# Mixture-of-experts stage: expert pairs share one half/half row block, the last 64 input rows of w1 run as a pair of row tiles, and the first expert's layer 1 goes by 128 rows

## The chip, the cores and the metric

One core of one Trainium2 chip runs the whole program in one launch. TensorE (PE) multiplies, VectorE (DVE), ScalarE (ACT) and GpSimd (POOL) work elementwise, SyncE (SP) and POOL issue DMAs. The metric is the time of one execution on the device in microseconds; lower is better. The kernel before was timed three times: 1001.54, 993.71 and 999.69 us, median 999.69 us.

## What is computed

Two parts follow each other. The first is a recurrent token mixer (RWKV-7) over 4 sequences of 768 tokens with 8 heads of 40; its output is reshaped to 3072 rows of 320. The second is a mixture of 8 experts: each row goes to the one expert with the largest gate value.

```python
x = attn_out.transpose(0, 2, 1, 3).reshape(B * S, H * D)      # 3072 x 320
logits = x @ w_gate                                           # 8 experts
expert_idx = np.argmax(logits, axis=1)
gate_w = probs[np.arange(N), expert_idx]                      # softmax weight of the chosen one
for e in range(E):                                            # rows sorted by expert
    h = np.maximum(x_sorted[lo:hi] @ w1[e], 0.0)              # 320 -> 1024
    y_sorted[lo:hi] = h @ w2[e]                               # 1024 -> 320
out = gate_w[:, None] * y_sorted[inv_perm]
```

All is float32. On the given inputs the argmax of the reference gives the eight experts 421, 323, 414, 388, 357, 423, 371 and 375 rows.

## The kernel before, in words

**The mixer** (lines 294 to 755) cuts the sequences into 24 units of work. Every piece of a unit is a `Step` with an engine, a cost and a rank, and the planner `in_order` writes the steps out in the order in which its costs say that they become ready; each engine's order is thereby fixed. PE's helper `mm` is line 385. The last steps of a unit scale its rows by the gate weight (lines 736 and 738, into `xs`) and store 128 rows of 320 to `x_rows` in DRAM (line 744, SP). POOL multiplies the inputs of a unit (lines 451 and 453).

**The router** (lines 758 to 862) runs when the mixer is done. It counts each row's place within its expert and turns it into a slot: expert e owns NJ = 4 blocks of 128 slots (CAP = 512 rows), rows beyond that go to overflow blocks behind the 32 regular ones. The lists `g_idx` (which row to gather into a slot) and `s_idx` (which output row the slot belongs to) come out of it.

**The experts** (lines 865 to 935) are run one after the other. `gather` fetches 128 rows per block with an indirect DMA on POOL. `turn` transposes a block on PE in three pieces (128, 128 and 64 of the 320 inputs) and DVE copies each piece into `xgT` (lines 882 and 883). `layer1` runs, for each of the 8 blocks of 128 hidden units, three matmuls that accumulate over the inputs, two with 128 rows and one with 64, each 512 columns wide (line 891); DVE and ACT take turns in applying the ReLU (lines 896 and 898). `layer2` gives each block of 128 rows 8 matmuls of 320 columns (line 904), a copy on ACT (line 909) and an indirect store on POOL (line 910). The profile shows two PE instructions per float32 matmul and one per transpose. `fetch` loads an expert's w1 and w2 (2.5 MB) through SP's queue into one of three buffers.

**Order.** Outside the mixer the tile framework's scheduler sets each engine's order from the program's order and its own estimates; semaphores hold what isn't ready. The overflow loop (line 938) runs only if an expert has more rows than CAP.

Of the kernel before, what the change touches and what calls it, by code (L numbers as in the profile page):

```python
# [8 lines left out]
F32 = mybir.dt.float32  # L9
# [5 lines left out]
AF = mybir.ActivationFunctionType  # L15
ALU = mybir.AluOpType
PSUM = bass.MemoryType.PSUM
# [6 lines left out]
def kernel(  # L24
# [21 lines left out]
    nc = tc.nc  # L46
    B, NW, _, D, _, NP, CW = packed.shape
    C = 64
# [20 lines left out]
    NJ = 4  # L69
    CAP = NJ * 128  # L70
    NX = -(-(N - CAP) // 128)
    NC = E * NJ + NX
    assert NC <= 128

# [56 lines left out]
    b1off = counted("b1off", [128, E], [[CAP, E]], -1)  # L131
    b2off = counted("b2off", [128, E], [[-CAP, E]], E * CAP - CAP)
# [25 lines left out]
    x_d = nc.dram_tensor("x_rows", (N, Dm), F32, kind="Internal").ap()  # L158
# [3 lines left out]
    def fetch(pool, w1, w2):  # L162
        t1 = pool.tile([128, DB, F], F32, name="w1")
        t2 = pool.tile([128, FB, Dm], F32, name="w2")
        full = Dm // 128
        nc.sync.dma_start(t1[:, :full, :], w1[: full * 128].rearrange("(a p) f -> p a f", p=128))
        if full < DB:
            nc.sync.dma_start(t1[: Dm - full * 128, full, :], w1[full * 128 :])
        nc.sync.dma_start(t2[:], w2.rearrange("(a p) d -> p a d", p=128))
        return t1, t2  # L170
# [124 lines left out]
    with tc.tile_pool(name="ring", bufs=1) as ring, \  # L295
# [42 lines left out]
        r_xs = Ring("xs", [NP, 2, D], 2, 2)  # L338
# [56 lines left out]
        def unit(u):  # L395
# [320 lines left out]
            def two():  # L716
                return psum[:, psx.at : psx.at + 2, : 2 * WX].rearrange("x b (i n) -> x b i n", i=2)
# [14 lines left out]
            for b in range(2):  # L732
                def scaled(e, b=b):
                    dst_, src_ = xs[:, 2 * b : 2 * b + 2], two()[:, b, :, :128].rearrange("x i (a d) -> x i a d", a=2)[:, :, :, :D]
                    if e == ACT:
                        nc.scalar.activation(dst_, src_, AF.Copy, scale=g[:, E:])
                    else:
                        nc.vector.tensor_scalar_mul(dst_, src_, g[:, E:])
                Step(late, ANY, 0.3, scaled, reads=[psx] + hg, writes=hxs[b : b + 1])

            def store(e):
                for q in range(2):
                    r0 = (2 * bh + q) * S + c * C
                    nc.sync.dma_start(x_d[r0 : r0 + C, :], xs[halves[q]].rearrange("x p a d -> x (p a d)"))
# [16 lines left out]
    with tc.tile_pool(name="rps", bufs=1, space=PSUM) as rps_pool:  # L761
# [103 lines left out]
    xg_pool = ctx.enter_context(tc.tile_pool(name="moe_x", bufs=3))  # L865
    wk_pool = ctx.enter_context(tc.tile_pool(name="moe_wk", bufs=2))
    mps_pool = ctx.enter_context(tc.tile_pool(name="moe_ps", bufs=3, space=PSUM))

    def gather(g):
        g["xg"] = xg_pool.tile([128, NJ, Dm], F32, name="xg")  # L870
        for j in range(g["n"]):
            nc.gpsimd.indirect_dma_start(  # L872
                out=g["xg"][:, j, :], out_offset=None,
                in_=x_d[:, :], in_offset=bass.IndirectOffsetOnAxis(ap=g["gi"](j), axis=0),
            )

    def turn(g):
        g["xT"] = wk_pool.tile([128, DB, CAP], F32, name="xgT")
        for j in range(g["n"]):
            tp = mps_pool.tile([128, DB, 128], F32, name="tp", bufs=2)  # L880
            for db, (d0, dsz) in enumerate(dch):
                nc.tensor.transpose(tp[:dsz, db, :], g["xg"][:, j, d0 : d0 + dsz], ident[:])  # L882
                nc.vector.tensor_copy(g["xT"][:dsz, db, j * 128 : (j + 1) * 128], tp[:dsz, db, :])  # L883

    def layer1(g):
        cols = g["n"] * 128
        g["h"] = wk_pool.tile([128, FB, CAP], F32, name="h_sb")
        for fb in range(FB):
            hp = mps_pool.tile([128, CAP], F32, name="hp")
            for db, (d0, dsz) in enumerate(dch):  # L890
                nc.tensor.matmul(  # L891
                    hp[:, :cols], lhsT=g["w"][0][:dsz, db, fb * 128 : (fb + 1) * 128],
                    rhs=g["xT"][:dsz, db, :cols], start=(db == 0), stop=(db == DB - 1),
                )
            if fb % 2 == 0:
                nc.vector.tensor_relu(g["h"][:, fb, :cols], hp[:, :cols])  # L896
            else:
                nc.scalar.activation(g["h"][:, fb, :cols], hp[:, :cols], AF.Relu)  # L898

    def layer2(g):  # L900
        for j in range(g["n"]):
            zp = mps_pool.tile([128, Dm], F32, name="zp", bufs=2)
            for fb in range(FB):
                nc.tensor.matmul(  # L904
                    zp[:], lhsT=g["h"][:, fb, j * 128 : (j + 1) * 128], rhs=g["w"][1][:, fb, :],
                    start=(fb == 0), stop=(fb == FB - 1),
                )
            zo = wk_pool.tile([128, Dm], F32, name="zo", bufs=3)
            nc.scalar.copy(zo[:], zp[:])  # L909
            ins_ = nc.gpsimd.indirect_dma_start(  # L910
                out=out[:, :], out_offset=bass.IndirectOffsetOnAxis(ap=g["si"](j), axis=0),
                in_=zo[:], in_offset=None, bounds_check=N - 1, oob_is_err=False,
            )
            ins_ = getattr(ins_, "ins", ins_)
            if g["apart"]:
                tc.declare_no_dep(ins_, group="rows_out", reason="disjoint rows")
                tc.add_to_no_dep_group("rows_out", ins_)

    def cols_of(t, c0):
        return lambda j: t[:, c0 + j : c0 + j + 1]  # L920

    groups = [dict(n=NJ, gi=cols_of(g_idx, e * NJ), si=cols_of(s_idx, e * NJ), apart=True) for e in range(E)]
    gather(groups[0])
    gather(groups[1])
    turn(groups[0])
    for e, g in enumerate(groups):
        if e + 2 < E:
            gather(groups[e + 2])
        g["w"] = weights.pop(e)
        layer1(g)  # L930
        if e + 1 < E:
            turn(groups[e + 1])
        layer2(g)
        if e + 2 < E:
            weights[e + 2] = fetch(w_pool, moe_w1[e + 2], moe_w2[e + 2])
# [3 lines left out]
    with tc.If(nx > 0):  # L939
        with tc.For_i(0, nx, 1) as i:  # L940
            ex = nc.sync.value_load(xe[0:1, bass.ds(i, 1)], min_val=0, max_val=E - 1)
            gi = wk_pool.tile([128, 2], I32, name="gi")
            nc.vector.tensor_copy(gi[:, 0:1], g_idx[:, bass.ds(i + E * NJ, 1)])
            nc.vector.tensor_copy(gi[:, 1:2], s_idx[:, bass.ds(i + E * NJ, 1)])
# [3 lines left out]
            g = dict(n=1, w=w, gi=lambda j: gi[:, 0:1], si=lambda j: gi[:, 1:2], apart=False)  # L948
            gather(g)
            turn(g)  # L950
            layer1(g)
            layer2(g)
# [34 lines left out]
```

## Time and profile before

| | |
|---|---|
| median of the runs | 999.69 us (993.71 to 1001.54) |
| the profiled execution | 996.33 us |
| its span, first to last instruction | 994.6 us |
| PE busy | 895.2 us (90%), 17804 matmul instructions |
| DVE, ACT, POOL busy | 393.3, 250.3, 172.9 us |
| mean granted TensorE clock | 0.966 |

The span begins with the first instruction and ends with the last one; 1.73 us of the profiled execution lie outside it. Busy shares are means over three stages (mixer to about 616 us, router to about 640 us, experts to the end), so they say little about one stage. In the tables "x" is a number of instructions, a value in square brackets is the idle time before an instruction and what ended it, and "issue" is waiting for nothing that the profile shows.

### The profile page before, as it was taken

To read this page: it belongs to the slowest core of one execution; us is meant where nothing else is said; L and a number is where in the kernel's file an instruction comes from. 1 tells how busy PE (TensorE), PEld (TensorE's weight loads), DVE (VectorE), ACT (ScalarE), POOL (GpSimd) and SP (SyncE) were. 2 spreads that over 40 slices of the span, in tenths; PEclk is the share of its full clock that TensorE was granted. 3 is DMA by queue.
4 is the path that set the end of the run, shared out by engine and by line. 5 is a ranking of instruction groups with operands and counts; after the bars stand their busy time and mean duration, and the time that the engine had idled before them with its cause. 6 is when DMAs were issued, how large, how long until landed. Compare 5 with 4: busy or idle time off the path is not lost. (4 is left out here: it accounts for less than half of the span.)

```text
span 994.6 us, 39246 instructions
## 1 busy us (share of the span) xinstructions
PE 895.2 (90%) x17804; PEld 651.6 (66%) x17804; DVE 393.3 (40%) x801; ACT 250.3 (25%) x508; POOL 172.9 (17%) x206
## 2 busy tenths in 40 slices
PE   0979999999999999989999995299999999999996
PEld 0877788888888888878888884136445363544534
DVE  6436566566555555555545542611201012010110
ACT  0334334333423333333423441001100000011000
POOL 8321202111201111111101000533022030100101
PEclk9999999999989999999989996599999999999998
DMA  5333313222212222222222001721122142212000
GB/s 157 81 78 69 75 43 74 57 57 67 63 37 55 61 57 56 60 54 61 59 48 53 14 11 33 237 62 49 60 89 93 61 123 79 76 60 68 20 0 21
DMA packets 132796, 64.18 MB, mean 65 GB/s; under 512 B 117009, under 2 KB 128275, under 8 KB 132628
## 3 DMA queue, kind: packets, MB, share of 16 engines
q1 hardware_dynamic: 127176, 51.97, 20.5%
q0 software_dynamic: 3072, 9.18, 3.1%
q8 instruction: 140, 2.29, 1.0%
q10 hardware_dynamic: 2380, 0.50, 0.2%
q14 instruction: 28, 0.23, 0.1%
HBM read 53.75 MB, written 9.18 MB: 63 GB/s over the span
## 5 line engine op out<-in xcount | busy, mean ns | idle before, releaser
L891 PE MATMUL hp<-xgT,w 128*128 128x512 f32 (+1 forms) x384 | 191.8, 629 | 0.0
L385 PE MATMUL ps<-X 64*64 64x64 f32 (+1 forms) x6144 | 151.4, 243 | 6.9 <-issue 3.5
L904 PE MATMUL zp<-w,h_sb 128*128 128x320 f32 x512 | 145.0, 433 | 0.0
L891 PEld LDWEIGHTS hp<-xgT,w 128*128 128x128 f32 (+1 forms) x384 | 63.4, 190 | 123.1 <-issue 122.0
L385 PEld LDWEIGHTS ps<-X 64*64 64x64 f32 x6144 | 128.0, 135 | 21.5 <-issue 13.4
L380 ACT COPY X<-ps 128x512 f32<-128x512 f32 x175 | 99.9, 586 | 122.8 <-PE ps L385 116.6
L896 DVE TENSOR_SCALAR h_sb<-hp 128x512 f32<-128x512 f32 x32 | 22.1, 692 | 247.2 <-PE hp L891 247.2
L904 PEld LDWEIGHTS zp<-w,h_sb 128*128 128x128 f32 x512 | 94.6, 191 | 34.5 <-issue 0.8
L451 POOL TENSOR_TENSOR KB<-KB,rv 128x512 f32<-128x512 f32 x48 | 56.6, 1200 | 209.4 <-DMA KB<-in_packed_dram 85.2
L382 DVE COPY X<-ps 128x512 f32<-128x512 f32 x89 | 61.5, 691 | 62.5 <-PE ps L385 62.4
L898 ACT ACTIVATE h_sb<-hp 128x512 f32<-128x512 f32 x32 | 19.1, 597 | 202.8 <-PE hp L891 202.8
L453 POOL TENSOR_TENSOR A<-A,q 128x512 f32<-128x512 f32 x24 | 28.4, 1183 | 231.6 <-PE ps L385 121.7
L910 POOL DMA_INDIRECT out_dram<-zo,s_idx x32 | 31.6, 989 | 181.4 <-ACT zo L909 180.2
L385 PE MATMUL ps<-X,ihalf 64*64 64x256 f32 x768 | 60.6, 377 | 1.1 <-issue 1.1
L436 DVE TENSOR_TENSOR_SCAN rv<-dec,ones 128x521 f32<-128x521 f32 x24 | 29.8, 1244 | 59.2 <-DMA dec<-in_packed_dram 57.7
L385 PE MATMUL ps<-R,Vu 64*128 64x64 f32 x768 | 50.9, 284 | 1.7 <-ACT Vu L644 1.6
L385 PE MATMUL ps<-A,KB 64*128 64x64 f32 x768 | 51.1, 286 | 0.0
L385 PEld LDWEIGHTS ps<-R,Vu 64*128 64x128 f32 x768 | 47.4, 196 | 5.0 <-ACT Vu L644 2.1
L872 POOL DMA_INDIRECT xg<-x_rows,g_idx x32 | 30.7, 959 | 108.6 <-PE tp L882 78.9
L385 PEld LDWEIGHTS ps<-A,KB 64*128 64x128 f32 x768 | 47.7, 198 | 2.3 <-POOL A L453 0.4
L909 ACT COPY zo<-zp 128x320 f32<-128x320 f32 x32 | 13.6, 425 | 134.4 <-PE zp L904 134.4
L467 DVE TENSOR_TENSOR GA<-ps,m_up 128x512 f32<-128x512 f32 x48 | 31.2, 685 | 39.2 <-PE ps L385 39.1
(174 smaller groups left out, 1127.5 us busy)
## 6 DMA issues: line engine op xcount, KB each, us to landing
w<-in_moe_w_dram SPq DMA_DIRECT2D x8, 1280.0 KB
w<-in_moe_w_dram SPq DMA_DIRECT2D x8, 1024.0 KB
KB<-in_packed_dram SPq DMA_DIRECT2D x188, 40.0 KB
dec<-in_packed_dram SPq DMA_DIRECT2D x96, 40.0 KB
V<-in_packed_dram SPq DMA_DIRECT2D x96, 40.0 KB
Vu<-in_packed_dram SPq DMA_DIRECT2D x96, 40.0 KB
x_rows<-xs SPq DMA_DIRECT2D x48, 80.0 KB
A<-in_packed_dram SPq DMA_DIRECT2D x92, 40.0 KB
```

The costliest lines, as they stand in the source:

```text
L380: nc.scalar.copy(dst, src)
L382: nc.vector.tensor_copy(dst, src)
L385: nc.tensor.matmul(out_, lhsT=lhsT, rhs=rhs, start=start, stop=stop, skip_group_check=True)
L436: Step(pre, DVE, 1.4, lambda e: nc.vector.tensor_tensor_scan(rv[:, : SEG * C1 + 1][:, ::-1], dec[:, ::-1], ones65[:, ::-1], 0.0, op0=ALU.m ...
L451: Step(pre, POOL, 1.25, lambda e, kb=kb, by=by: nc.gpsimd.tensor_tensor(kb, kb, by, op=ALU.mult), reads=hrv, writes=hKB[i : i + 1])
L453: Step(pre, POOL, 1.22, lambda e: nc.gpsimd.tensor_tensor(Aq[:], Aq[:], q3[:, :, :C], op=ALU.mult), reads=hq, writes=hA)
L467: Step(u, DVE, 0.69, lambda e, s=s, ps=ps: nc.vector.tensor_tensor(GA[:, s], psum[:, ps.at + s, :].rearrange("x (p q j) -> x p q j", p=NP, ...
L872: nc.gpsimd.indirect_dma_start(out=g["xg"][:, j, :], out_offset=None, in_=x_d[:, :], in_offset=bass.IndirectOffsetOnAxis(ap=g["gi"](j), ax ...
L891: nc.tensor.matmul(hp[:, :cols], lhsT=g["w"][0][:dsz, db, fb * 128 : (fb + 1) * 128], rhs=g["xT"][:dsz, db, :cols], start=(db == 0), stop= ...
L896: nc.vector.tensor_relu(g["h"][:, fb, :cols], hp[:, :cols])
L904: nc.tensor.matmul(zp[:], lhsT=g["h"][:, fb, j * 128 : (j + 1) * 128], rhs=g["w"][1][:, fb, :], start=(fb == 0), stop=(fb == FB - 1),)
L910: ins_ = nc.gpsimd.indirect_dma_start(out=out[:, :], out_offset=bass.IndirectOffsetOnAxis(ap=g["si"](j), axis=0), in_=zo[:], in_offset=Non ...
```

## The change

**Blocks.** NJ becomes 3 and CAP 448: an expert owns three blocks of its own and half of a fourth, which it shares with its partner (experts 0 and 1, 2 and 3, ...). A pair has PB = 7 blocks instead of 8, all four pairs 28 instead of 32. The router's slot arithmetic gets a second threshold.

**Rows of 384.** `x_rows` is 384 wide: POOL copies the last 64 inputs of each row behind them, so that a transposed block holds these 64 twice, in partitions 0 to 63 and 64 to 127. The last 64 rows of w1 are loaded into a tile of their own, `w1c`, even hidden blocks in the lower partitions and odd ones in the upper.

**Layer 1** takes two hidden blocks at a time: four matmuls with 128 rows, then two with 64 rows, one in each half of the array's rows. It is 448 columns wide; expert 0's is cut into four passes of 128, 128, 128 and 64 columns.

**Layer 2** of the shared block lets the first expert's 64 rows fill output partitions 0 to 63 and the second's 64 to 127, by turns. `turn` copies a whole block with one DVE instruction (two for the shared block). Work buffers are three deep instead of two, `hp` has four PSUM buffers instead of three, `xg` holds a pair's seven blocks, two deep.

```diff
-    NJ = 4
-    CAP = NJ * 128
+    NJ = 3
+    PB = 2 * NJ + 1
+    CAP = NJ * 128 + 64
...
-        t1 = pool.tile([128, DB, F], F32, name="w1")
+        t1 = pool.tile([128, DB - 1, F], F32, name="w1")
+        t3 = pool.tile([128, FB // 2, 128], F32, name="w1c")
...
+        for i in range(2):
+            nc.sync.dma_start(
+                t3[i * 64 : (i + 1) * 64], w1[Dm - 64 :].rearrange("p (k i f) -> i p k f", i=2, f=128)[i],
+            )
...
+            Step(late, POOL, 0.2, lambda e: nc.gpsimd.tensor_copy(xs[:, Dm:], xs[:, Dm - 64 : Dm]), reads=hxs[1:2], writes=hxs[2:3])
...
-        gx = sm_pool.tile([128, E, NT], F32)
-        nc.vector.tensor_scalar(gx[:], slot[:], scalar1=CAP + 0.5, scalar2=None, op0=ALU.is_ge)
-        nc.vector.tensor_tensor(gx[:], gx[:], b2[:].unsqueeze(2).to_broadcast([128, E, NT]), op=ALU.mult)
-        nc.vector.tensor_add(slot[:], slot[:], gx[:])
+        nc.vector.tensor_sub(b2[:], b2[:], b3off[:])
+        gx = sm_pool.tile([128, 2, E, NT], F32)
+        for i, (above, by) in enumerate(((NJ * 128, b3off), (CAP, b2))):
+            nc.vector.scalar_tensor_tensor(
+                gx[:, i], in0=slot[:], scalar=above + 0.5, in1=by[:].unsqueeze(2).to_broadcast([128, E, NT]),
+                op0=ALU.is_ge, op1=ALU.mult,
+            )
+        for i in range(2):
+            nc.vector.tensor_add(slot[:], slot[:], gx[:, i])
...
+    def turn(xg, j, *to):
+
+        tp = mps_pool.tile([128, DB, 128], F32, name="tp", bufs=2)
+        for db in range(DB):
+            nc.tensor.transpose(tp[:, db, :], xg[:, j, db * 128 : (db + 1) * 128], ident[:])
+        for xT, r0, n, c0 in to:
+            nc.vector.tensor_copy(xT[:, :, c0 : c0 + n], tp[:, :, r0 : r0 + n])
+
+    def layer1(w, xT, h, c0, c1):
+        for fb in range(0, FB, 2):
+            hps = []
+            for i in range(2):
+                hp = mps_pool.tile([128, CAP], F32, name="hp")
+                hps.append(hp)
+                for db in range(DB - 1):
+                    nc.tensor.matmul(
+                        hp[:, : c1 - c0], lhsT=w[0][:, db, (fb + i) * 128 : (fb + i + 1) * 128], rhs=xT[:, db, c0:c1],
+                        start=(db == 0), stop=False,
+                    )
+            for i in range(2):
+                hf = slice(i * 64, (i + 1) * 64)
+                nc.tensor.matmul(hps[i][:, : c1 - c0], lhsT=w[1][hf, fb // 2, :], rhs=xT[hf, DB - 1, c0:c1], start=False, stop=True)
+            nc.vector.tensor_relu(h[:, fb, c0:c1], hps[0][:, : c1 - c0])
+            nc.scalar.activation(h[:, fb + 1, c0:c1], hps[1][:, : c1 - c0], AF.Relu)
+
+    def layer2(si, *parts, apart=True):
+
+        zp = mps_pool.tile([128, Dm], F32, name="zp", bufs=2)
         for fb in range(FB):
+            r0 = 0
+            for w, h, c0, n in parts:
                 nc.tensor.matmul(
+                    zp[r0 : r0 + n], lhsT=h[:, fb, c0 : c0 + n], rhs=w[2][:, fb, :], start=(fb == 0), stop=(fb == FB - 1),
...
+    turns(0)
+    xgs[1] = gathers(1)
+    for e in range(E):
+        k, i = divmod(e, 2)
+        w = weights[e]
+        h = hs[e] = wk_pool.tile([128, FB, CAP], F32, name="h_sb")
+
+        for c0 in (range(0, CAP, 128) if e == 0 else (0,)):
+            layer1(w, xTs[e], h, c0, min(c0 + 128, CAP) if e == 0 else CAP)
+        if e + 1 < E:
+            turns(e + 1)
+        if i == 1 and k + 2 < E // 2:
+            xgs[k + 2] = gathers(k + 2)
+        for j in range(NJ):
+            layer2(col(k * PB + i * NJ + j), (w, h, j * 128, 128))
+        if i == 1:
+            layer2(col(k * PB + 2 * NJ), *((weights[x], hs[x], NJ * 128, 64) for x in (e - 1, e)))
```

How the instructions stand, at three places. First PE where the experts begin: `tp` is a transposed block, `hp` a layer-1 result, `w_223` (before) and `w_227` (now) the first 256 rows of w1 of expert 0. Before:

```order
L882 MATMUL tp<-ident,xg 128x128 x4
L882 MATMUL tp<-ident,xg 64x128 x2
L882 MATMUL tp<-ident,xg 128x128 x4
L891 MATMUL hp<-xgT,w_223 128x512
L882 MATMUL tp<-ident,xg 64x128 x2
L891 MATMUL hp<-xgT,w_223 128x512 x23
```

Now:

```order
L895 MATMUL tp<-ident,xg 128x128 x9
L906 MATMUL hp<-xgT,w_227 128x128
L895 MATMUL tp<-ident,xg 128x128 x3
L906 MATMUL hp<-xgT,w_227 128x128 x3
L912 MATMUL hp<-xgT,w1c 128x128 x2
```

All four blocks (12 transposes) still stand ahead of layer 1, but for one matmul; layer 1 itself is cut into 128-column pieces.

Second PE at an odd expert (expert 1): its last hidden blocks, the next expert's transposes and layer 2, where `zp` is a layer-2 result and `w_229` and `w_10741` are w2 of experts 0 and 1. Before:

```order
L891 MATMUL hp<-xgT,w_10709 128x512 x24
L882 MATMUL tp<-ident,xg 128x128 x2
L904 MATMUL zp<-w_10710,h_sb 128x320
L882 MATMUL tp<-ident,xg 128x128 x2
L904 MATMUL zp<-w_10710,h_sb 128x320
L882 MATMUL tp<-ident,xg 64x128 x2
```

Now:

```order
L906 MATMUL hp<-xgT,w_10739 128x448 x4
L912 MATMUL hp<-xgT,w1c 128x448 x2
L895 MATMUL tp<-ident,xg 128x128 x6
L922 MATMUL zp<-w_10741,h_sb 128x320
L895 MATMUL tp<-ident,xg 128x128 x6
L922 MATMUL zp<-w_10741,h_sb 128x320 x23
L922 MATMUL zp<-w_229,h_sb 64x320
L922 MATMUL zp<-w_10741,h_sb 64x320
```

The 64-row matmuls stand two by two, transposes go in sixes with one layer-2 matmul between, and the shared block alternates the two experts.

Third POOL in the mixer, two units of work, where `KB` and `A` are scaled inputs of a unit. Before:

```order
L451 TENSOR_TENSOR KB_160<-KB_160,rv_169 128x512 x2
L453 TENSOR_TENSOR A_152<-A_152,q_172 128x512
L451 TENSOR_TENSOR KB_158<-KB_158,rv_168 128x512 x2
L453 TENSOR_TENSOR A_150<-A_150,q_170 128x512
L451 TENSOR_TENSOR KB_159<-KB_159,rv_169 128x512 x2
```

Now:

```order
L459 TENSOR_TENSOR KB_164<-KB_164,rv_173 128x512 x2
L461 TENSOR_TENSOR A_156<-A_156,q_176 128x512
L459 TENSOR_TENSOR KB_162<-KB_162,rv_172 128x512 x2
L751 COPY xs_216<-xs_216 128x64
L461 TENSOR_TENSOR A_154<-A_154,q_174 128x512
L751 COPY xs_217<-xs_217 128x64
```

The copy of the 64 inputs stands among the unit's multiplications, and the store of `x_rows` waits for it. PE's order in the mixer is as it was.

## Rows read from the trace of the kernel before

**Rows 1.** Windows: us, then busy us of each engine, granted clock, DMA share, GB/s.

```profile
647.00:650.00 3.00, 3.00 (x6) 1.15 (x5) 0.49 (x2) 0.00 (x0) 2.39 (x3) 0.53 0.50 130
650.00:671.30 21.30, 21.30 (x44) 6.80 (x42) 2.77 (x4) 1.79 (x3) 5.10 (x6) 1.00 0.19 52
713.63:985.10 271.47, 271.47 (x809) 135.84 (x808) 34.08 (x96) 26.40 (x52) 38.23 (x39) 1.00 0.22 69
985.10:994.60 9.50, 0.00 (x1) 0.00 (x0) 0.00 (x0) 0.42 (x1) 0.98 (x1) 0.64 0.01 1
```

**Rows 2.** Timeline of PE, two experts: start, duration in us, engine, line, instruction.

```profile
690.00 23.70 PE L891 MATMUL hp<-xgT,w 128*128 128x512 f32 x48
...
732.32 23.70 PE L891 MATMUL hp<-xgT,w 128*128 128x512 f32 x48
```

**Rows 3.** Timeline of ACT, two blocks of the last expert's layer 2.

```profile
976.57 0.42 ACT L909 COPY zo<-zp 128x320 f32<-128x320 f32 x1 [3.93 <-PE zp L904]
980.88 0.42 ACT L909 COPY zo<-zp 128x320 f32<-128x320 f32 x1 [3.88 <-PE zp L904]
```

**Rows 4.** Timeline of PE's weight loads in layer 1; two instructions a matmul.

```profile
690.86 0.19 PEld L891 LDWEIGHTS hp<-xgT,w 128*128 128x128 f32 x1 [0.24 <-issue]
691.81 0.29 PEld L891 LDWEIGHTS hp<-xgT,w 64*128 64x128 f32 x2 [0.76 <-issue]
...
693.83 0.19 PEld L891 LDWEIGHTS hp<-xgT,w 128*128 128x128 f32 x1 [0.24 <-issue]
```

**Rows 5.** Timeline of PE in the mixer; rows*columns of the tile, moving shape.

```profile
316.47 0.61 PE L385 MATMUL ps<-GA,ihalf 64*64 64x256 f32 x8
316.90 0.29 PE L385 MATMUL ps<-N,GA 64*64 64x64 f32 x8
...
317.96 2.00 PE L385 MATMUL ps<-R,Vu 64*128 64x64 f32 x32
319.89 1.09 PE L580 MATMUL ps<-ident,Vu 128*128 128x128 f32 x8
...
322.85 1.65 PE L385 MATMUL ps<-ZU,nKB 128*64 128x104 f32 x32
324.42 0.66 PE L571 MATMUL ps<-ident,V 128*128 128x128 f32 x4
```

**Rows 6.** Timeline of PE, two narrow windows: the last two, and the last one, of those 32.

```profile
319.67 0.29 PE L385 MATMUL ps<-R,Vu 64*128 64x64 f32 x2
...
319.69 0.27 PE L385 MATMUL ps<-R,Vu 64*128 64x64 f32 x1
```

**Rows 7.** Chain of work: start, us, what; last gather of expert 0.

```profile
640.68 3.31 DMA xg<-x_rows,g_idx
```

**Rows 8.** Timeline of PE: that block's transposes, and the end of layer 1.

```profile
644.12 0.66 PE L882 MATMUL tp<-ident,xg 128*128 128x128 f32 x2 [0.63 <-DMA xg<-x_rows,g_idx]
...
671.30 0.44 PE L882 MATMUL tp<-ident,xg 128*128 128x128 f32 x2
```

**Rows 9.** Timeline of DVE in the router.

```profile
618.68 0.36 DVE L764 TENSOR_TENSOR sc<-lgn,lmin 128x192 f32<-128x192 f32 x1 [3.02 <-DMA x_rows<-xs]
...
623.26 0.25 DVE L813 TENSOR_SCALAR gx<-slot 128x192 f32<-128x192 f32 x1
...
624.69 0.36 DVE L815 TENSOR_TENSOR slot<-slot,gx 128x192 f32<-128x192 f32 x1
```

**Rows 10.** Timeline of POOL and ACT: a small POOL copy; a unit's scaling and POOL's next work.

```profile
1.69 0.23 POOL L99 COPY ihalf<-ident 64x64 f32<-64x64 f32 x1
...
306.67 0.40 ACT L736 ACTIVATE xs<-ps,g 128x160 f32<-128x160 f32 x1
...
316.13 2.34 POOL L451 TENSOR_TENSOR KB<-KB,rv 128x512 f32<-128x512 f32 x2 [11.12 <-DMA KB<-in_packed_dram]
```

**Rows 11.** Groups of DVE from 600 us on: xcount, busy us, mean ns, idle before.

```profile
L896 DVE TENSOR_SCALAR h_sb<-hp 128x512 f32<-128x512 f32 x32 | 22.1, 692 | 247.2 <-PE hp L891 247.2
```

**Rows 12.** Timeline of SP's queue: a later expert's w2.

```profile
732.52 0.37 SPq L169 DMA_DIRECT2D w<-in_moe_w_dram  x1
```

More of the change, by code (lines that the diff above doesn't have):

```diff
@@ L862 @@
         nc.vector.tensor_copy(s_idx[:], tb[:])
[L865 to L887, printed above, removed]
+    xg_pool = ctx.enter_context(tc.tile_pool(name="moe_x", bufs=2))
@@ new lines, with gather @@
+    wk_pool = ctx.enter_context(tc.tile_pool(name="moe_wk", bufs=3))
+    mps_pool = ctx.enter_context(tc.tile_pool(name="moe_ps", bufs=4, space=PSUM))
+    def gather(xg, j, gi):
+        nc.gpsimd.indirect_dma_start(
+            out=xg[:, j, :], out_offset=None, in_=x_d[:, :], in_offset=bass.IndirectOffsetOnAxis(ap=gi, axis=0),
+        )
[5 more added lines that the diff above has]
+            nc.vector.tensor_copy(xT[:, :, c0 : c0 + n], tp[:, :, r0 : r0 + n])
@@ L895, in layer1 @@
[L895 to L913, printed above, removed]
-            ins_ = getattr(ins_, "ins", ins_)
-            if g["apart"]:
-                tc.declare_no_dep(ins_, group="rows_out", reason="disjoint rows")
-                tc.add_to_no_dep_group("rows_out", ins_)
@@ new lines, in layer2 @@
+                    skip_group_check=True,
+                )
+                r0 += n
+        zo = wk_pool.tile([128, Dm], F32, name="zo")
+        nc.scalar.copy(zo[:], zp[:])
+        ins_ = nc.gpsimd.indirect_dma_start(
+            out=out[:, :], out_offset=bass.IndirectOffsetOnAxis(ap=si, axis=0),
+            in_=zo[:], in_offset=None, bounds_check=N - 1, oob_is_err=False,
+        )
+        if apart:
+            ins_ = getattr(ins_, "ins", ins_)
+            tc.declare_no_dep(ins_, group="rows_out", reason="disjoint rows")
+            tc.add_to_no_dep_group("rows_out", ins_)
@@ new lines, in gathers, with col, turns @@
+    def gathers(k):
+        xg = xg_pool.tile([128, PB, DX], F32, name="xg")
+        for j in (*range(NJ), 2 * NJ, *range(NJ, 2 * NJ)):
+            gather(xg, j, g_idx[:, k * PB + j : k * PB + j + 1])
+        return xg
+    def col(b):
+        return s_idx[:, b : b + 1]
+    xgs = {0: gathers(0)}
+    xTs, hs = {}, {}
+    def turns(e):
+        k, i = divmod(e, 2)
+        if i == 0:
+            for x in (e, e + 1):
+                xTs[x] = wk_pool.tile([128, DB, CAP], F32, name="xgT")
+        for j in range(NJ):
+            turn(xgs[k], i * NJ + j, (xTs[e], 0, 128, j * 128))
+        if i == 0:
+            turn(xgs[k], 2 * NJ, *((xTs[e + a], 64 * a, 64, NJ * 128) for a in range(2)))
@@ L947 @@
             )
[L948 to L952, printed above, removed]
+            xg = xg_pool.tile([128, PB, DX], F32, name="xg")
+            xT = wk_pool.tile([128, DB, CAP], F32, name="xgT")
+            h = wk_pool.tile([128, FB, CAP], F32, name="h_sb")
+            gather(xg, 0, gi[:, 0:1])
+            turn(xg, 0, (xT, 0, 128, 0))
+            layer1(w, xT, h, 0, 128)
+            layer2(gi[:, 1:2], (w, h, 0, 128), apart=False)
 _OUTS = [((3072, 320), 'float32')]
```

56 lines of the change are left out of this document (22 added, 34 removed).

## The prediction

> **What bounds the kernel now.** I read the windows first, because the busy shares are means over three stages. From about 650 us to 985 us PE has no idle time and runs at the full granted clock (1.00, the 2.4 GHz level), while DVE, ACT, POOL and the DMAs are far from full [rows 1]. So in the expert stage the end is set by PE's own stream: whatever is taken out of it is gained one for one, as long as the others keep up. The timeline of PE shows the period of one expert: 732.32 - 690.00 = 42.32 us, of which layer 1 is 23.7 us [rows 2] and the rest, 18.6 us, is layer 2 with the next expert's transposes. Behind the last matmul lie 9.5 us of copy, store and ending [rows 1], which nothing here touches.
>
> **Unit prices.** Two copies of finished layer-2 blocks stand 4.31 us apart [rows 3]. A block is 8 matmuls of 2 instructions and 320 columns: 0.269 us each, 0.84 ns per column and instruction. A 512-column instruction is then 0.430 us. In layer 1 the same weight load comes back after 693.83 - 690.86 = 2.97 us [rows 4], which is one hidden block with 6 instructions, 2.58 us of streaming. The remaining 0.39 us are its two changes of shape (128 rows to 64 and back): before the 64-row load the load queue sits idle for 0.76 us, so weights aren't loaded ahead across a change. One change costs 0.2 us. The 18.6 us less 4 x 4.31 leave 1.4 us for 12 transposes, 0.12 us each.
>
> **Layer 1 of experts 1 to 7.** Two hidden blocks take 8 instructions of 448 columns (0.376 us each, 3.01 us), one pair of 64-row matmuls and two changes (0.4 us). The price of the pair is the open one. One after the other it would be 4 x 0.376 = 1.50 us; with both row tiles at work together it is 0.75 us. Nothing in the trace runs such a pair at this width. The nearest rows are the mixer's. Tiles of 64x64 with 256 columns: 8 instructions from 316.47 to 316.90 [rows 5], 0.43 us, which is exactly two streams of 256 columns, so four tiles, two of them above each other, worked at once. Tiles of 64x128 with 64 columns: 32 instructions in 319.89 - 317.96 = 1.93 us [rows 5], no better than one after the other (32 x 0.054 = 1.72 and a change). That speaks against overlap at first sight, but every such instruction also loads 128 columns of weights, and full-width transposes with 128 columns, right behind, need about as long per load. The last two of them decide for me: one starts at 319.67 and the other at 319.69 [rows 6], 0.02 us apart, which two streams of 0.054 us in one queue could not. I take 0.75 us and keep 1.50 for the range. Then two hidden blocks are 4.16 us and an expert 16.6 us instead of 23.7: 7 x 7.1 = **49.7 us less**.
>
> The Trainium skill, "TensorE: Matmul & The Clock Gate", section "Measured speedup vs the span model", gives only 3.07 times for four row tiles, 77% of full overlap. By that a pair would be about 0.98 us, an estimate, and the sum 938. The trace's 0.43 us for four tiles is full overlap [rows 5], so I stay with it and keep partial overlap as a rival.
>
> **Layer 2.** A pair of experts had 8 blocks and has 7. The shared one runs two 64-column tiles by turns. In the mixer 32 instructions of that kind with 104 columns took 324.42 - 322.85 = 1.57 us [rows 5], 1.37 without the change of shape, where one after the other they would take 2.80. So they overlap fully, and the shared block costs a block's 4.31 us and two changes, 4.7. Saved: 2 x 4.31 - 4.7 = 3.9 us a pair, **15.7 us in all**.
>
> **Transposes.** There are 84 instead of 96, 1.4 us less. But six now come in a row with two buffers, and DVE, still at the ReLU of the last pair (0.69 us for 512 columns [rows 11]), has to copy 384 columns (about 0.54 us by the same rate) before the third block can be turned. One layer-2 matmul of 0.54 us stands between. I put 0.2 us of waiting on each of 7 experts, 1.4 us: **together nothing**.
>
> **Expert 0.** The change's words suggest that it starts with the rows that have arrived. By the order on PE it can't: the transposes of the fourth block stand ahead of all but one of its matmuls, and that block's gather lands last, at 640.68 + 3.31 = 643.99 [rows 7]. Before, layer 1 ended at 671.30 [rows 8], 27.3 us after that. Now: three transposes, 0.8 us (two took 0.66 us at that clock [rows 8]); then four passes. In a pass of 128 columns an instruction is 0.107 us, so two hidden blocks are 10 x 0.107 and two changes, 1.47 us, and a pass 5.9 us. For the pass of 64 columns streaming alone would give 3.7 us; I take 5.9, since the 64-column tiles above went at the pace of their loads. Four passes: 23.5 us, where one pass of 448 would be 16.6. The granted clock is 0.53 between 647 and 650 us and 1.00 after [rows 1], so the first 5 us run at the 1.2 GHz level and lose 2.5 us. In all 26.8 us against 27.3: **0.5 us less**. The cut costs about what the narrower layer 1 would have brought here.
>
> **Ahead of the experts.** The router's first instruction waits for the last store of x_rows [rows 9], and that store now waits for a POOL copy: 0.3 us (a 64x64 copy takes 0.23 [rows 10]). Two router instructions of 0.25 and about 0.36 us become two of about 0.36, plus an addition of 0.36 [rows 9] and a subtraction on 8 columns: 0.6 us. Longer rows in the gather: 0.1 us. **1.0 us more.** Inside the mixer the copy is hidden: ACT's scaling ends at 307.07 and POOL's next multiplication starts at 316.13, held by its own DMA [rows 10]. Without that 9 us of cover each of 24 copies would cost 0.3 us, 7 us in all.
>
> **What must not become late.** The weights: an odd expert's w2 now waits until the shared block of the pair before is done, but is needed only a whole even expert and one layer 1 later, 47 us; before, an expert's w2 was asked for at 732.52 [rows 12] and the DMAs stood at 22% [rows 1]. The third pair's gathers now wait on POOL for expert 1's transposes, with expert 0's stores queued behind them for some 9 us; three output buffers cover that until expert 1's layer 2. Both ReLUs of a pair come at once, each under 0.7 us, and four buffers leave 4 us.
>
> **Sum.** -49.7 - 15.7 + 0 - 0.5 + 1.0 = -64.9 us. The profiled execution took 996.33 us, 0.3% under the median of the runs (999.69): 996.33 - 64.9 = **931 us**. With the change priced at both ends (the 64-column pass at 3.7 us, no transpose wait, no POOL wait), the forecast's own range is 923 to 937.
>
> **Rivals.**
> Row tiles in part or not at all together. For it: the 1.93 us. Against: four tiles at once, and the two starts. Not at all: 28 pairs x 0.75 and 16 narrow ones x 0.21, 24.5 us, 956 us; in between, about 943. Chance 0.12, half of it at each. The skill's 77% is of this kind.
> The cut expert 0 never gets the full clock. Before, the clock rose under dense 512-column streams; now short streams and a change every 0.5 us or so stand there. Against: the mixer's tiles run at the full rate with shorter streams [rows 5]. The other 21 us would take twice as long: 952 us. Chance 0.08.
> Column tiles one after the other: 4 x 4.3 us, 949 us. The 1.57 us speak against it. Chance 0.03.
> Slower than before: the pairs and shape changes keep TensorE at 1.2 GHz through layer 1 of experts 1 to 7. Its 116 us would double, to about 1047 us; it decides from some 65 us of doubled work on, over half of layer 1. For it: the clock did stay low for as long as PE had gaps [rows 1]. Against: layer 1 already changes shape twice every 2.97 us [rows 4] and holds 1.00. Chance 0.02.
> That rows overflow into the loop I leave out: the fullest expert has 423 rows, under 448.
>
> **Chances.** The forecast has 0.72, the rivals 0.25, and 0.03 are for something cheaper still. Faster by over 1% (10 us, about what a measurement of this kernel tells from none): all but the last rival and an unnamed stall, 0.97; within 1%: 0.01; slower: 0.02. The range of 921 to 954 leaves out rows one after the other and the slow case, and reaches down to an expert 0 without its clock loss and its waits.
>
> **What would show it.** Layer 1 of an expert takes 16.6 us in PE's timeline, two 64-row matmuls of a pair start within 0.05 us, finished blocks stay 4.3 us apart with the shared one at 4.7, a pair of experts has a period near 67 us, expert 0's layer 1 ends 26.8 us after its last gather. Layer 1 at 19.6 us would mean row tiles one after the other; idle time of PE behind a DMA or a semaphore in the expert stage would mean that one of the covers failed.

## The result and the profile after

The changed kernel's median is 934.12 us (928.01 to 944.22), beside 1000.62 us for the kernel before: ratio 0.933, 95% interval 0.926 to 0.940. (Ratios and their intervals leave out executions more than 1.5% behind the fastest of their kernel; medians don't.) The forecast was 931 us, its range 921 to 954. The profiled execution took 928.01 us, its span is 926.3 us, 68.3 us less than before; the forecast said 64.9 us less.

Windows of the changed kernel: the beginning of expert 0, the rest of its layer 1, the other experts' matmuls, the end (us, busy us of each engine, granted clock, DMA share, GB/s).

```profile
640.50:649.30 8.80, 7.67 (x32) 6.18 (x32) 2.59 (x6) 0.28 (x1) 6.67 (x8) 0.50 0.56 156
649.40:670.60 21.20, 21.20 (x174) 18.07 (x173) 3.88 (x14) 3.72 (x14) 3.95 (x5) 1.00 0.19 53
684.60:917.30 232.70, 232.70 (x864) 126.69 (x862) 27.98 (x52) 25.84 (x53) 31.32 (x32) 1.00 0.22 73
917.30:926.30 9.00, 0.01 (x2) 0.00 (x0) 0.00 (x0) 0.42 (x1) 0.98 (x1) 0.78 0.01 2
```

As in [rows 1], PE is busy without a gap from expert 1 on, at a granted clock of 1.00. The timeline of PE shows where layer 1 of experts 1 and 2 begins and what follows it:

```profile
684.57 3.17 PE L906 MATMUL hp<-xgT,w 128*128 128x448 f32 x8
687.67 1.02 PE L912 MATMUL hp<-xgT,w1c 64*128 64x448 f32 x4
688.62 3.27 PE L906 MATMUL hp<-xgT,w 128*128 128x448 f32 x8
...
701.09 0.87 PE L895 MATMUL tp<-ident,xg 128*128 128x128 f32 x6
...
720.12 3.27 PE L906 MATMUL hp<-xgT,w 128*128 128x448 f32 x8
...
736.75 0.88 PE L895 MATMUL tp<-ident,xg 128*128 128x128 f32 x6
...
750.76 1.67 PE L906 MATMUL hp<-xgT,w 128*128 128x448 f32 x4
...
767.28 0.88 PE L895 MATMUL tp<-ident,xg 128*128 128x128 f32 x6
```

Layer 1 takes 701.09 - 684.57 = 16.52 us (16.63 behind an odd expert: 736.75 - 720.12), where [rows 2] showed 23.7 (23.63 to the next transpose at 713.63, [rows 1]). A pair of 64-row matmuls takes 688.62 - 687.67 = 0.95 us to the next start. The rest of a period is 19.03 us behind an odd expert (720.12 - 701.09) and 14.01 us behind an even one. Two experts take 767.28 - 701.09 = 66.19 us.

A narrow window of PE's timeline answers to [rows 6]: two instructions, each up to 0.64 us long, lie within 0.65 us, so they started together.

```profile
687.67 0.65 PE L912 MATMUL hp<-xgT,w1c 64*128 64x448 f32 x2
```

ACT's copies of finished blocks answer to [rows 3]; the last of these blocks is the shared one:

```profile
711.51 0.42 ACT L928 COPY zo<-zp 128x320 f32<-128x320 f32 x1 [3.92 <-PE zp L922]
715.81 0.42 ACT L928 COPY zo<-zp 128x320 f32<-128x320 f32 x1 [3.88 <-PE zp L922]
720.31 0.42 ACT L928 COPY zo<-zp 128x320 f32<-128x320 f32 x1 [4.07 <-PE zp L922]
```

Ordinary blocks stay 4.30 us apart, the shared one takes 4.50 us.

Expert 0 and the router: PE's first transposes and the end of expert 0's layer 1, POOL's new copy, and the router's first instruction on DVE (for [rows 8 to 10]). In a pass of 128 columns two hidden blocks take 651.39 - 649.88 = 1.51 us.

```profile
640.51 0.87 PE L895 MATMUL tp<-ident,xg 128*128 128x128 f32 x3 [5.11 <-DMA xg<-x_rows,g_idx]
...
649.88 1.16 PE L906 MATMUL hp<-xgT,w 128*128 128x128 f32 x8
...
651.39 1.16 PE L906 MATMUL hp<-xgT,w 128*128 128x128 f32 x8
...
670.60 0.88 PE L895 MATMUL tp<-ident,xg 128*128 128x128 f32 x6
```

```profile
615.25 0.24 POOL L751 COPY xs<-xs 128x64 f32<-128x64 f32 x1 [21.59 <-DVE xs L747]
```

```profile
618.51 0.36 DVE L776 TENSOR_TENSOR sc<-lgn,lmin 128x192 f32<-128x192 f32 x1 [3.33 <-DMA x_rows<-xs]
```

### The profile page after: what moved, and what is told of

Read it like the earlier page. It is cut to its first block, busy times and chain, and to the rows that moved or that the text cites. A ratio compares the mean times of both kernels' runs of the same rounds, so it can differ in the third digit from the quotient of the medians.

```text
span 926.3 us, 39472 instructions
## 1 busy us (share of the span) xinstructions
PE 829.6 (90%) x17936; PEld 648.6 (70%) x17936; DVE 383.9 (41%) x751; ACT 249.0 (27%) x516; POOL 170.4 (18%) x224
## 4 chain that ended last, share of the span: by engine, by line
PE 40%; issue 34%; DMA 9%; POOL 6%; DVE 5%; SPq 3%; ACT 1%; POOLq 0%; DVEq 0%; ACTq 0%
PE ps L393 36%; DMA dec<-in_packed_dram 8%; PE ps L588 3%; POOL out_dram L929 3%; SPq L428 3%; POOL xg L887 3%; DVE q L452 1%; PE ps L579 1%; ACT TF L388 1%; DVE rv L444 1%; DVE xT L707 0%; DVE ZU L674 0%; DVE oh_c L852 0%; DVE ST L606 0%; DVE oh_r L859 0%
## 5 line engine op out<-in xcount | busy, mean ns | idle before, releaser
L922 PE MATMUL zp<-w,h_sb 128*128 128x320 f32 (+1 forms) x512 | 123.8, 433 | 0.0
L913 DVE TENSOR_SCALAR h_sb<-hp 128x448 f32<-128x448 f32 (+2 forms) x44 | 21.9, 497 | 218.7 <-PE hp L912 218.7
L906 PE MATMUL hp<-xgT,w 128*128 128x448 f32 (+2 forms) x352 | 111.4, 460 | 0.0
L922 PEld LDWEIGHTS zp<-w,h_sb 128*128 128x128 f32 (+1 forms) x512 | 80.6, 177 | 37.5 <-issue 2.4
L906 PEld LDWEIGHTS hp<-xgT,w 128*128 128x128 f32 x352 | 57.9, 196 | 48.8 <-issue 46.6
L929 POOL DMA_INDIRECT out_dram<-zo,s_idx x28 | 27.6, 987 | 185.0 <-ACT zo L928 183.8
L914 ACT ACTIVATE h_sb<-hp 128x448 f32<-128x448 f32 (+2 forms) x44 | 19.4, 442 | 152.7 <-PE hp L912 152.7
L393 PE MATMUL ps<-ZU,nKB 128*64 128x104 f32 (+1 forms) x768 | 41.3, 260 | 6.0 <-DVE ZU L674 5.7
L393 PEld LDWEIGHTS ps<-ZU,nKB 128*64 128x64 f32 x768 | 35.9, 142 | 15.2 <-issue 11.6
```

Of the source, the lines that this page charges most:

```text
L393: nc.tensor.matmul(out_, lhsT=lhsT, rhs=rhs, start=start, stop=stop, skip_group_check=True)
L906: nc.tensor.matmul(hp[:, : c1 - c0], lhsT=w[0][:, db, (fb + i) * 128 : (fb + i + 1) * 128], rhs=xT[:, db, c0:c1], start=(db == 0), stop=False,
L922: nc.tensor.matmul(zp[r0 : r0 + n], lhsT=h[:, fb, c0 : c0 + n], rhs=w[2][:, fb, :], start=(fb == 0), stop=(fb == FB - 1), skip_group_check ...
L929: ins_ = nc.gpsimd.indirect_dma_start(out=out[:, :], out_offset=bass.IndirectOffsetOnAxis(ap=si, axis=0), in_=zo[:], in_offset=None, bound ...
```

## The experiments

The length of the mixer differs by some 10 us from one execution to the next. Its clock falls to 0.50 several times for 3 to 10 us, at other places each time; how much of the difference that makes wasn't worked out. So each single execution is judged from the first transpose of expert 0 to the end of the span, which I call the **stage**: 354.6 us before (639.99 to 994.6), 285.8 us in the changed kernel. The first transpose before:

```profile
639.99 0.45 PE L882 MATMUL tp<-ident,xg 128*128 128x128 f32 x1 [5.02 <-DMA xg<-x_rows,g_idx]
```

**One row tile after the other.** All 64-row tiles in partitions 0 to 63; the load of `w1c` changes to match (not shown here), nothing else:

```diff
-nc.tensor.matmul(hps[i][...], lhsT=w[1][hf, fb // 2, :], rhs=xT[hf, DB - 1, c0:c1], ...)
+nc.tensor.matmul(hps[i][...], lhsT=w[1][:64, fb + i, :], rhs=xT[:64, DB - 1, c0:c1], ...)
```

> The changed kernel, but the last 64 rows of w1 of both hidden blocks lie in partitions 0 to 63, so the two 64-row matmuls of a pair use the same half of the array. Number of instructions, columns and shape changes stay. Theory (in the changed kernel the two row tiles work at the same time): two hidden blocks take 4.9 us instead of 4.16 us at 448 columns, layer 1 of an expert 19.5 us instead of 16.5, and the span grows by 28 x 0.75 + 3.4 for expert 0, from 926.3 to about 951 us. Rival (the pair never overlapped, the gain came from fewer columns and fewer shape changes): 4.16 us and 926 us as before.

983.03 us, a stage of 333.2 us. Its PE timeline in expert 1:

```profile
722.07 1.77 PE L908 MATMUL hp<-xgT,w1c 64*128 64x448 f32 x4
723.77 3.27 PE L903 MATMUL hp<-xgT,w 128*128 128x448 f32 x8
```

A pair costs 1.70 us instead of 0.95: 0.75 us more, exactly two streams of 448 columns. So in the changed kernel the row tiles overlap fully. Two experts take 810.53 - 738.48 = 72.05 us instead of 66.19, so 2.93 us more each. But that explains 8 x 2.93 = 23 us of the 47 by which the stage grew. The rest is in expert 0, where the clock rose only at 707.93:

```profile
651.20:702.20 51.00, 50.35 (x197) 43.76 (x195) 5.58 (x19) 3.99 (x15) 8.51 (x9) 0.50 0.15 40
719.00:733.00 14.00, 14.00 (x36) 6.18 (x35) 1.32 (x3) 1.51 (x3) 0.98 (x1) 1.00 0.03 12
```

PE was busy in 50.35 of 51 us and yet ran at 0.50. This is my second rival, in a kernel that differs from the changed one only in the partitions of those tiles and in their load.

**The old order with 448 columns.** Each hidden block takes its two 128-row matmuls and then its own 64-row one.

```diff
-for fb in range(0, FB, 2): ...  # four matmuls, then the pair
+for fb in range(FB): ...        # two matmuls, then one with 64 rows
```

> Layer 1 in the order of the kernel before at the new width: per hidden block two matmuls with 128 rows and then one with 64 rows, always in partitions 0 to 63; blocks, layer 2 and all else as changed. Theory (overlap of row tiles 0.75 us and two spared shape changes of 0.2 us per two hidden blocks): two hidden blocks 12 x 0.376 + 4 x 0.2 = 5.3 us, layer 1 21.2 us, span about 926.3 + 32 + 10 for expert 0 = 968 us. Rival (the narrower 448 columns are the main gain of layer 1): layer 1 close to 16.5 us and a span within 10 us of 926.

1003.16 us, no faster than before: two experts take 75.20 us, 4.5 us more an expert than in the changed kernel, and expert 0's layer 1 stays at the low clock, 59 us long (653.26 to 712.59):

```profile
653.20:712.60 59.40, 59.03 (x198) 46.11 (x196) 5.58 (x19) 3.99 (x15) 8.51 (x9) 0.50 0.12 34
```

Layer 1 of expert 1 takes 749.23 - 728.16 = 21.07 us here. So of the 7.1 us that the change takes out of an expert's layer 1, the 448 columns bring 23.63 - 21.07 = 2.56 us and the pairs the other 4.5: 2.9 by overlap (the run above) and the rest by fewer changes of shape. What the later experts gained was eaten by expert 0, whose way from the first transpose to the end of layer 1 took 62.4 us instead of 31.3.

**Column tiles apart.** In the shared block the first expert's 8 matmuls, then the second's:

```diff
-for fb in range(FB):
-    for w, h, c0, n in parts:
+for w, h, c0, n in parts:
+    for fb in range(FB):
```

> The shared block's 8 matmuls of the first expert come first and then the 8 of the second, instead of by turns; everything else as changed. Theory (column tiles overlap because neighbours in the queue use different halves of the columns): the shared block takes 8.8 us instead of 4.5, span 926.3 + 4 x 4.3 = 943 us. Rival (a 64-column tile is cheaper by itself, whatever stands next to it): 4.5 us and 926 us.

ACT's copies around the shared block, and PE at its middle:

```profile
733.66 0.43 ACT L928 COPY zo<-zp 128x320 f32<-128x320 f32 x1 [3.88 <-PE zp L922]
741.40 0.43 ACT L928 COPY zo<-zp 128x320 f32<-128x320 f32 x1 [7.31 <-PE zp L922]
```

```profile
735.71 2.10 PE L922 MATMUL zp<-w,h_sb 128*64 128x320 f32 x10
```

The shared block takes 7.74 us instead of 4.50, so it is the alternation that pays. It isn't the full 2 x 4.31: where the first expert's tile hands over to the second's, ten instructions fit into 2.10 us, which one after the other need 2.8. 958.98 us, a stage of 306.0 us: 13 us are the shared blocks, 7 us are again expert 0.

**Expert 0 in one pass.**

```diff
-for c0 in (range(0, CAP, 128) if e == 0 else (0,)):
-    layer1(w, xTs[e], h, c0, min(c0 + 128, CAP) if e == 0 else CAP)
+layer1(w, xTs[e], h, 0, CAP)
```

> Expert 0's layer 1 in one pass of 448 columns instead of four; everything else as changed. Theory (the cut brings no earlier start and costs 7 us of short streams and shape changes): layer 1 of expert 0 takes 16.6 us plus about 2 us lost to the 1.2 GHz clock, it ends 6 us earlier against its last gather, span about 920 us. Rival (the cut pays by starting with rows that have arrived): the span is 926 us or more.

From the first transpose to the end of expert 0's layer 1 it is 674.84 - 650.78 = 24.06 us instead of 30.09; the stage is 279.4 us, 6.4 us less. The whole execution took 931.93 us, since it came to that transpose 10 us later. The cut costs 6 us even when the clock behaves.

**Passes as rows arrive.** Each pass is asked for right behind its block.

```diff
-turns(0)
+for j in range(NJ + 1):
+    turn(...)                      # block j
+    layer1(weights[0], xTs[0], hs[0], j * 128, min(j * 128 + 128, CAP))
```

> The first pass of expert 0 is asked for right behind the block that it reads, where the change asks for it behind all four. Theory (the PE scheduler had already put passes 0 and 1 ahead of what it could, and each pass of 128 columns costs 6.04 us at the full clock against 16.5 us for one pass of 448): from the first transpose to the end of layer 1 of expert 0 the time is 30.1 us less the 2 to 4 us that PE no longer waits for the rows, so 26 to 28 us; that is still 2 to 4 us more than the 24.1 us of one pass. Rival (the work ahead of the last rows runs at 1.2 GHz anyway and gives nothing back, or the clock rises later because PE works in pieces): 30 us or more. From the first transpose to the end of the span 282 to 284 us by the theory, 286 or more by the rival (285.8 in the changed kernel).

The rival's side, and more: layer 1 of expert 0 ends 38.25 us after the first transpose, the stage is 295.6 us. PE started 1.9 us after its first transpose, as asked, but then stood still for 4.42 us, and the clock fell twice. Here is what PE waited for, on ACT:

```profile
658.11 0.28 ACT L914 ACTIVATE h_sb<-hp 128x128 f32<-128x128 f32 x1 [2.77 <-PE hp L912]
665.90 0.28 ACT L914 ACTIVATE h_sb<-hp 128x128 f32<-128x128 f32 x1 [7.51 <-remote]
```

"remote" means that nothing in this trace released the instruction. The ReLU at 665.90 belongs to the third pair, which ended on PE at 658.20 (a start at 657.71 and 0.49 us), so it began 7.7 us behind its input:

```profile
657.71 0.49 PE L912 MATMUL hp<-xgT,w1c 64*128 64x128 f32 x4
...
664.13 1.22 PE L906 MATMUL hp<-xgT,w 128*128 128x128 f32 x4 [4.42 <-issue]
```

The two ReLUs of that pair ended at 664.08 (DVE) and 666.18 (ACT), and PE went on at 664.13 and 666.23: it stood for the buffers that they free. The second fall of the clock, at 686.22, was another: it came in the 64-column pass, behind matmuls without a gap since 666.23.

**Pairs back to back.** One pass for expert 0, and every other pair of hidden blocks takes its 64-row pair first, so that two pairs stand together and the shape changes half as often.

```diff
+first = fb % 4 == 2
+if first: narrow()      # the two 64-row matmuls
 ...                     # four 128-row matmuls
-narrow()
+if not first: narrow()
```

> One pass for expert 0, and the pairs of half-row tiles stand two and two together: every other pair of hidden blocks takes its half rows first. Theory (a change of tile shape costs about 0.1 us each time, the drain and the load that can not be hidden): 5 changes fewer... 10 instead of 20 in layer 1 of an expert, so 16.5 us becomes 15.6 us, eight times, -7 us beside the run with one pass alone; from the first transpose to the end of the span 272 to 273 us against 279.4. Rival (the gap in the starts is the wait for the two half-row results, not the change of shape): 279 us, layer 1 stays at 16.5 us.

The PE timeline of expert 1:

```profile
689.62 3.17 PE L916 MATMUL hp<-xgT,w 128*128 128x448 f32 x8
692.73 1.77 PE L907 MATMUL hp<-xgT,w1c 64*128 64x448 f32 x8
694.43 6.28 PE L916 MATMUL hp<-xgT,w 128*128 128x448 f32 x16
...
705.46 0.82 PE L895 MATMUL tp<-ident,xg 128*128 128x128 f32 x6
```

Two pairs take 1.70 us to the next start, where they took 2 x 0.95; layer 1 is 15.84 us, two experts 64.59 us instead of 66.19 (705.46 to 770.05), 0.80 us an expert. The stage is 273.3 us. The theory's gain came, but by another count than it wrote: an expert has 8 changes of shape and now 4, at 0.2 us each.

**One row tile after the other, one pass.** The first experiment with expert 0 uncut.

> The half-row tiles all in partitions 0 to 63 (one after the other), and one pass for expert 0. In the run with the same tiles and the cut expert 0 the clock stayed at 1.2 GHz until 707.93. Theory (the passes of 128 columns keep it low, when no two tiles run together): with one pass the clock rises within 12 us of the first transpose, and the stage from the first transpose to the end is 279.4 us plus 8 times 2.93 us, so 303 us (333.2 with the cut). Rival (the lone half-row tiles keep it low, whatever the number of columns): the clock stays low through layer 1 of expert 0, 303 plus 19 = 322 us. Second rival (it depends on something ahead of the experts, as the clock in the mixer does, and varies from one execution to the next): either of the two.

Now the clock is up 7.0 us after the first transpose, and the stage is 301.7 us:

```profile
652.40:659.30 6.90, 5.49 (x17) 3.32 (x18) 2.85 (x6) 0.00 (x0) 5.07 (x7) 0.50 0.56 160
659.40:678.10 18.70, 18.70 (x47) 7.94 (x45) 2.45 (x4) 1.63 (x3) 5.43 (x6) 1.00 0.31 79
```

The theory's 303 us: lone row tiles by themselves don't hold the clock down. That the cut does is one execution against one here; the count over all executions is further below.

**Work ahead of the rows.** As the pairs back to back, with TensorE busy while the first rows are fetched.

```diff
+for _ in range(12):
+    nc.tensor.matmul(idle[:], lhsT=oh_r[:, NT - 1, :], rhs=oh_r[:, NT - 4 :, :], start=True, stop=True)
```

> As the run with pairs back to back, and TensorE computes 12 matmuls of 128x512 half-precision numbers, whose result nobody reads, while the first rows of expert 0 are being fetched (635.4 to 640.5 in the changed kernel). Theory (the clock is at 1.2 GHz until TensorE has been busy for a while, and the work of expert 0 that is done before it rises takes twice as long): the clock rises some 5 us earlier in relation to the first transpose, and from the first transpose to the end of the span the time is 2 to 3 us less than without them. Rival (that work is hidden by the wait for the rows, whose last block lands 3.5 us behind the first transpose): less than 1 us.

Expert 0's layer 1 ended 22.26 us after the first transpose instead of 23.54, the stage is 272.0 us: between the two. The clock rose 0.3 us after the first transpose began (652.24), fell again at 655.65 while PE waited for rows, and rose at 659.07.

**The changed kernel again**, timed on the same chip as the two that follow.

> The changed kernel as it stands, looked at a second time. In the runs with the same cut of expert 0 the clock was late or fell again (rose at 707.93 and 715.91, or rose, fell and rose again), in the changed kernel it rose 8.8 us behind the first transpose and stayed. Theory (the cut leaves it open when the clock rises, and a stall of the ReLU engines in the first pass can delay it): the stage from the first transpose to the end of the span is 286 us again, or 10 to 20 us longer. Rival (a pair that runs together always brings the clock up): 285 to 287 us. Ratio to the kernel before 0.93 by either, or 0.945 by the theory's late clock.

Median 939.57 us, ratio 0.937 (0.931 to 0.944). The profiled execution took 945.12 us with a stage of 295.6 us, nearly 10 us more than in the first: the theory. Its PE timeline in expert 0:

```profile
658.05 0.49 PE L912 MATMUL hp<-xgT,w1c 64*128 64x128 f32 x4
659.54 0.71 PE L906 MATMUL hp<-xgT,w 128*128 128x128 f32 x4 [0.99 <-DVE h_sb L913]
660.93 0.71 PE L906 MATMUL hp<-xgT,w 128*128 128x128 f32 x4 [0.68 <-issue]
661.57 0.49 PE L912 MATMUL hp<-xgT,w1c 64*128 64x128 f32 x4
664.54 2.08 PE L906 MATMUL hp<-xgT,w 128*128 128x128 f32 x8 [2.48 <-DVE h_sb L913]
```

and its DVE:

```profile
659.19 0.29 DVE L913 TENSOR_SCALAR h_sb<-hp 128x128 f32<-128x128 f32 x1 [4.02 <-PE hp L912]
664.19 0.49 DVE L913 TENSOR_SCALAR h_sb<-hp 128x128 f32<-128x128 f32 x2 [4.71 <-remote]
```

The ReLU at 664.19 belongs to the pair that ended at 658.54, so it came 5.6 us late. PE ran out of free result buffers and stood for 4.2 us, and from 663.05 to 676.71 the clock was at 0.50 again (eight such instructions take 2.08 us instead of 1.16). Expert 0's layer 1 ended 39.87 us after the first transpose.

**The two best, timed**: the pairs back to back, and the same with work ahead of the rows.

> The run with one pass for expert 0 and the pairs back to back, timed. From its stage (273.3 us from the first transpose to the end of the span, against 285.8 in the changed kernel) 12.5 us less than the changed kernel in the mean, if the mixers ahead are equally long: ratio to the kernel before about 0.92, against 0.933. Rival (what the first look gained is a matter of one execution): 0.93.

> The run with work for TensorE ahead of the first rows, timed. Its stage was 272.0 us against 273.3 us without that work: 1 to 1.5 us less, a ratio of 0.917 to 0.92 to the kernel before. Rival (the waits of expert 0 for its rows hide it): the same as without.

921.58 and 917.36 us; ratios 0.915 (0.906 to 0.925) and 0.917 (0.911 to 0.923). Both beat the change, with intervals that don't meet its 0.931 to 0.944. By the single executions above, 6.4 us of the stage are the one pass and 6.1 the order of the pairs. Between them there is no difference: the work ahead of the rows gains nothing that can be measured, as its rival had it (expert 0's layer 1 ended 22.78 us after the first transpose without it here, 23.72 us with it).

**The next rows later.** The fetches of experts 2 and 3 begin when layer 1 of expert 0 is done; the cut is kept.

```diff
+nc.gpsimd.tensor_copy(xg[:, :, 0], behind)     # behind = a part of expert 0's last hidden block
```

> The changed kernel with expert 0 cut as it is, but the row fetches of experts 2 and 3 begin only when layer 1 of expert 0 is done (in the changed kernel they are under way beside it, and in four looks with that cut the ReLUs stood 4 to 7.5 us behind results that were there, each time until about the last of these fetches landed). Theory (these transfers hold up what the ReLU engines need): no such wait in the first passes, the clock rises once and stays, and from the first transpose to the end of the span it is 285 to 287 us; four times within a few us of each other. Rival (the ReLU engines wait for their instructions or something else that has nothing to do with these transfers): the wait is there again in the look, 290 to 296 us, and a median like the changed kernel's second set of runs. A look without the wait does not settle it by itself, since two of six looks with the cut had none.

Four executions within 4 us (937.62 to 941.38), median 939.22 us, ratio 0.938 (0.931 to 0.945). No late ReLU in the profiled one, and a stage of 288.7 us. Its windows in expert 0 show another loss:

```profile
656.00:676.40 20.40, 20.40 (x167) 17.35 (x165) 3.66 (x13) 3.50 (x13) 0.00 (x0) 1.00 0.00 1
676.50:683.30 6.80, 6.80 (x26) 5.48 (x26) 2.03 (x5) 0.40 (x2) 3.06 (x4) 0.50 0.58 196
```

PE had no gap in 20.4 us, and the clock fell all the same, in the last blocks of the 64-column pass. Whether the transfers make the ReLUs late stays open. For it: the wait was away here, and in all five executions with a ReLU more than 2 us late the last late one began 3.2 to 3.4 us after the last of these fetches was issued (664.19 against 660.94 in the changed kernel again; a fetch takes 3.2 us to land in the first one, by the median). Against: in the first execution of the changed kernel the fetches were issued until 653.62, beside its ReLUs, and none was late; and the median here is no better. (The 4 to 7.5 us of the expectation are idle times of the ReLU engines; their inputs had been there for 2 to 8 us of them. It counts two executions without a wait, but in the old order with 448 columns one ReLU, at 666.56, came 2.8 us late.)

## Why the prediction was right, step by step

Each row: the step, the forecast, the first profiled execution.

| step | forecast | measured |
|---|---|---|
| to the router's first instruction | +0.3 | -0.2 (618.51 against 618.68) |
| router and first gather | +0.7 | +0.7 (22.00 us to the first transpose instead of 21.31) |
| expert 0, first transpose to the end of layer 1 | -0.5 | -1.2 (30.09 instead of 31.31) |
| layer 1 of experts 1 to 7 | -49.7 | -49.4 (7 x 23.63 less 4 x 16.52 and 3 x 16.63) |
| layer 2 and transposes | -15.7 | -17.7 |
| end | 0 | -0.5 (8.97 instead of 9.50) |
| sum | -64.9 | -68.3 |

The sum is right because its large terms are; that the medians differ by 66.5 us, nearer to the forecast than the profiled execution, is in part luck. The profiled execution is the fastest of the four. Nearly all the smaller gains came out larger than forecast, 3.4 us in sum, and the clock that falls again in other executions of this kernel, which costs time, was not in the sum.

**Layer 1.** The price of a pair, 0.75 us, was the open one, read from the mixer's four tiles in 0.43 us and from two starts 0.02 us apart [rows 5, 6]. It holds: 0.95 us to the next start, against 1.70 us when the tiles are made to run one after the other; the 0.2 us besides are a change of shape. The Trainium skill's 3.07 times for four row tiles of 32 rows ("TensorE: Matmul & The Clock Gate", "Measured speedup vs the span model") would give an estimate of 0.98 us and, with that change, 1.18; the measurement decides for full overlap here.

**Layer 2.** The shared block costs 4.50 us and not 4.7: two changes of shape cost 0.2 us together there, which is 0.8 us over four pairs. The transposes were put at nothing, 1.4 us less against seven waits of 0.2 us. Behind an even expert 9 of them take 14.01 - 3 x 4.31 = 1.08 us, 0.12 each and no wait; behind an odd one 12 take 19.03 - 3 x 4.31 - 4.50 = 1.60, at most 0.16 us of waiting. So they came out 1.2 us less, and both together are the 2.0 us by which this term was too small.

**Expert 0.** The step "the cut costs about what the narrower layer 1 would have brought here" held in one execution and not as a rule. The price of a pass was right: two hidden blocks in 1.51 us (forecast 1.47), 6.0 us for 128 columns, 5.6 for 64, and layer 1 ended 25.9 us behind the start of the last block's transposes at 644.70 (forecast 26.8 behind its landing). What the sum left out is that such passes leave little slack. I had put the late clock at a chance of 0.08, as an all-or-nothing case of 21 us. The executions show it in parts: of seven profiled executions with the cut, one kept the clock once it was up. Two never got it in layer 1 (both with row tiles one at a time, though PE was 99% busy), three lost it after a late ReLU, one in the last pass (as did one of the three, a second time). The six profiled ones without the cut and the kernel before all had it up within the first two hidden blocks and kept it through layer 1. The words "the clock did stay low for as long as PE had gaps [rows 1]" were too simple as well: from 647 to 650 us those rows show no gap and a clock of 0.53. The Trainium skill ("TensorE: Matmul & The Clock Gate", "What's actually happening") says that the clock is held back by default and that activity of PE releases it; the 50.35 busy us at 0.50 in the first experiment disagree with the plain reading of that. What it is about these passes, the runs don't tell: they are narrow, and they change the shape twice in every 1.51 us.

**Why a late ReLU should hurt the cut alone** (worked out, not run). In a pass of 128 columns two hidden blocks are done every 1.51 us, so four result buffers are full after 3 us. With 448 columns two blocks take 4.15 us, and four buffers cover 8. In the uncut kernels no ReLU was more than 2 us late and none stopped PE, so a longer wait is untested there. Why ACT and DVE begin late, with their inputs there, isn't settled.

**Ahead of the experts** was right: the router's part came out as summed: 0.6 us up to the first gather's issue, 0.1 from there to PE. The store behind POOL's copy starts 0.26 us after the copy does, but the mixer varies by far more than that.

## What to carry to other kernels

Two row tiles, or two column tiles, of TensorE that stand next to each other in its queue run fully together in this kernel, even in float32. For row tiles it takes different partitions (the first experiment), for column tiles the order by turns (the third); pairs that stand together save changes of shape as well. Cutting a matmul stage into narrow passes so as to start early cost twice here: in the passes themselves, and in the slack that the engines behind them have. Where a kernel's clock varies ahead of the stage in question, compare from a mark inside the program to the end, and take a second profile before calling one the rule.

## What the runs showed of the hardware

- The granted clock stayed at 0.50 for 51 us in which PE was busy 50.35 us (narrow passes, row tiles one at a time), and fell from 1.00 to 0.50 behind 20.4 us without a gap (64-column pass, fetches delayed).
- ACT and DVE began some ReLUs 2 to 8 us after their inputs were there, in five of the seven profiled executions with the cut, several of them with no releaser in the trace, until about when the last of the next experts' row fetches landed.
- In the float32 stream a change between 128-row and 64-row tiles costs about 0.2 us (8 changes an expert, then 4: 0.80 us less), one between 128 and 64 columns about 0.1 us (4.50 us for the shared block, 4.30 for others).
- At the seam of two column tiles ten instructions ran in 2.10 us: matmuls for the second tile start before the first tile's are all done.
